# Turning q on quarters of TensorE's array: the first eight attention jobs of a fused retention and SwiGLU kernel

## The chip, the cores and the metric

The kernel runs on one core of one Trainium2 chip. A core has TensorE (matrix products; PE in the profile, PEld for its weight loads), VectorE (DVE), ScalarE (ACT), GpSimd (POOL) and SyncE (SP, which here only issues DMAs). The metric is device time in microseconds, as the median of several executions. Lower is better. Everything is fp32; one product is two passes through the array, and so two weight loads and two matmuls in the trace, and a transpose on TensorE is one of each.

## The reference

The first half is causal retention over 8 batches and 8 heads, with 576 tokens and 64 features a head. The second half is RMS-normalised SwiGLU over the 4608 tokens that result.

```python
scores = (1.0 / np.sqrt(D_)) * np.matmul(q, k.transpose(0, 1, 3, 2))
gamma = 1.0 - 2.0 ** (-5.0 - np.arange(H))
rel = pos[:, None] - pos[None, :]
Dmat = np.where(rel >= 0, gamma[:, None, None] ** rel[None, :, :], 0.0)
x = np.matmul(scores * Dmat, v)              # (B, H, S, D) -> (B*S, H*D) = (4608, 512)

xn = x / np.sqrt(np.mean(x * x, axis=-1, keepdims=True) + 1e-06) * rms_g
g = xn @ w_gate                              # 512 -> 1536
out = (g * (1.0 / (1.0 + np.exp(-g))) * (xn @ w_val)) @ w_out
```

## The kernel before

**Attention.** A job is one batch and one pair of heads (e = 0 and 1): 32 jobs, job j for batch j // 4. The pair fills the 128 partitions: 64 features of one head, 64 of the other. Retention is computed in chunks of 64 tokens, nine a job. The products of features need q and k with features on partitions (qT and kT), while memory has tokens on rows, so every job has to turn them.

For the jobs from the ninth on, `prepare` does that on VectorE. For the first eight, `turn(j)` does it on TensorE. The changed function is `turn`, with `load_tails`, which loads what it turns last. The 576 tokens of a head are four full tiles of 128 and a tail of 64:

- `load_first` loads the full tiles of q so that partition p holds tokens 4p to 4p + 3 of each head; those of k so that a tile has 128 consecutive tokens. Four lots of q, k and v go to free parts of `h`, the other four to free parts of `ring`.
- `load_tails` loads the tails of q, k and v of one or several heads into the tile `vi`, each on partitions 0 to 63 and in its own columns. `TAILS` has four such loads: heads 0 and 1 of batch 0 (issued by ScalarE's queue), the other six (by SyncE's), and the same for batch 1.
- `turn(j)` takes three PSUM banks. For q it multiplies each tile of each head by the identity (L236): 128 rows of the array and 64 columns, e choosing the column half. The result of tile c goes to every fourth column from c on, so that the tokens come out in order. For k it transposes the tiles of both heads at once (L230, 128x128). The two tails are transposed into a third bank (L245, 64 rows). ScalarE copies each of the four results to SBUF: two of 512 columns (L241), two of 64 (L252).

After `turn(j)` comes `slot(j)`, with TensorE's work in this order: `values(j-1)` (L379), `scores(j)` (L292), `states(j)` (L315) and `carried(j-1)` (L399). All of these are products of 64x64. `scores` puts the head on the row half of the array and the chunk's parity on the column half, so that four products are on four quarters, with a PSUM bank for each row half. `carried` adds to what `values` left, head e on the row half e and the column half e, and so uses two quarters. VectorE weights the scores with the decay (`weigh`, L328), sums the states (`sums`, L341) and scales what `carried` left into x (L425). ScalarE scales v (`scale_v`, L273), copies half of the states (L349) and computes squares for the norm (L458).

**Order.** The order of the first two units of 512 tokens is written out by hand in `PLAN`: T is `turn`, S is `slot`, V is `scale_v`, C is `close` (values and carried of the last of the eight jobs). N is `norm_1` (L481: means of squares, one column wide; then a power on GpSimd), D is `diagonals` (L495, ScalarE), X is `norm_2` (L546, which spreads the roots to all rows, and L548). U is `up_plain` (L704: products 512 columns wide with w_gate and w_val), and a and w are steps that make weights out of the 64-bit inputs on ScalarE and VectorE. The first steps are T0 V0 S0 T1 V1 S1 T2 and so on; N0 comes after S6, D0 after that and before T7, X0 after T7, then S7, the first U, C7. `LOADS` is the order of the DMAs; SyncE issues nearly all of them.

**The rest.** Later units (512 tokens each, from the third on) run their up- and down-projections as block products with fewer multiplications (`up`, L644; `across`, L814), with the weight blocks read back from DRAM into `ring`, and with jobs nine to 32 between them.

Of the kernel before, what the change touches and what calls it, by code (L numbers as in the profile page):

```python
# [10 lines left out]
F32 = mybir.dt.float32  # L11
# [3 lines left out]
P = 128  # L15
L = P // 2
# [28 lines left out]
def kernel(  # L45
# [11 lines left out]
    nc = tc.nc  # L57
    B, H, S, D = q.shape
    NTOK, DM = out.shape
    DFF = moe_w_gate.shape[1]  # L60
    NHP = H // 2
    NF = DFF // P
    NC = S // L
    NFULL = S // P
    TAIL = S - NFULL * P
# [16 lines left out]
    att = ctx.enter_context(tc.tile_pool(name="att", bufs=2))  # L82
# [6 lines left out]
    def bank(name):  # L89
        return banks.tile([P, 512], F32, tag="b", name=name)  # L90
# [13 lines left out]
    ident = const.tile([P, P], F32, name="ident")  # L104
# [18 lines left out]
    h = const.tile([P, NF, U], F32, name="h")  # L123
# [3 lines left out]
    NV = 4 * 7 * P  # L127
    vi = const.tile([P, NV + 2 * 4 * NK * P], F32, name="vi")
# [20 lines left out]
    st = [{} for _ in jobs]  # L149
# [33 lines left out]
    def load_tails(i, queue):  # L183

        b, heads = TAILS[i]
        for n, (nm, src) in enumerate((("qt", q), ("kt", k), ("vt", v))):
            at = NV + (3 * b + n) * DM
            t = vi[:TAIL, at : at + DM].rearrange("p (h d) -> p h d", d=D)
            cut = slice(heads[0], heads[-1] + 1)
            queue.dma_start(  # L190
                out=t[:, cut], in_=src[b, cut, NFULL * P :].rearrange("h p d -> p h d")
            )
            for hp in range(heads[0] // 2, heads[-1] // 2 + 1):
                st[b * NHP + hp][nm] = t[:, 2 * hp : 2 * hp + 2]

    def load_kv(j):

# [14 lines left out]
    def warm_up(n, width=P):  # L212

        if not warm_of:
            warm_of[0] = bank("warm")
        for _ in range(n):
            nc.tensor.matmul(
                warm_of[0][:, :width], lhsT=ones, rhs=ones[:, :1].to_broadcast([P, width]),
                start=True, stop=True,
            )  # L220

    def turn(j):

        d = st[j]
        n = NFULL
        for nm in "qk":
            ps = bank(f"turn_{j}_{nm}")
            for c in range(n):
                if nm == "k":
                    nc.tensor.transpose(  # L230
                        out=ps[:, c * P : c * P + P],
                        in_=d["k"][:, c].rearrange("p e d -> p (e d)"), identity=ident,
                    )
                    continue
                for e in range(2):
                    nc.tensor.matmul(  # L236
                        ps[side(e), c : n * P : n], lhsT=d["q"][:, e, c], rhs=ident,
                        start=True, stop=True,
                    )
            t = d[nm + "T"] = att.tile([P, S], F32, tag=nm + "T", name=f"{nm}T_{j}")  # L240
            nc.scalar.copy(out=t[:, : n * P], in_=ps[:, : n * P])  # L241
        last = bank(f"turn_{j}_t")
        for i, nm in enumerate("qk"):
            o = slice(i * TAIL, i * TAIL + TAIL)
            nc.tensor.transpose(  # L245
                out=last[:, o], in_=d[nm + "t"].rearrange("p e d -> p (e d)"),
                identity=ident[:TAIL, :TAIL],
            )
        warm_up(j == 0, 2 * P)
        for i, nm in enumerate("qk"):  # L250
            o = slice(i * TAIL, i * TAIL + TAIL)
            nc.scalar.copy(out=d[nm + "T"][:, NFULL * P :], in_=last[:, o])  # L252

    def prepare(j):

# [23 lines left out]
    def side(i):  # L279
        return slice(i * L, i * L + L)  # L280
# [304 lines left out]
    at = AT_SUMS  # L585
    for kind, u, n in pieces:
        size = UP if kind == "up" else OUT
        if at + size > RING:
            at = AT_SETS if kind == "out" and u < 2 else 0
# [754 lines left out]
```

## Time and profile before

| | |
|---|---|
| median of 3 runs | 1104.73 us (1101.4 to 1110.42) |
| span of the profiled execution | 1104.5 us, 24454 instructions |
| PE busy | 1091.5 us (99%), 10102 matmuls and as many loads |
| DVE, ACT, POOL busy | 751.7, 339.7, 458.0 us |
| granted clock of TensorE, mean | 0.995 |
| up to 57.38 us (first L704): PE busy | 50.51 us of 57.38, clock 0.91 |
| DMA moved | 243.60 MB, 221 GB/s in the mean |

The profile has no time of the profiled execution other than its span; the span lies 0.2 us under the median of the runs. A row of the timeline reads: start, time taken, engine, line, operation, written tile <- read tiles, shape of the array or operands, number of instructions, and in brackets the engine's idle time before it with what ended it. "issue" means that the engine waited for nothing that the profile shows. A matmul's row includes the time in which its result drains; the rate of a group is read from the starts of it and of the next.

Of a job's turn and slot in a stretch without stops (job 3, 23.27 to 27.85 us), TensorE spends 1.03 us on q's products, 0.59 on k's transposes, 0.26 on the tails', 0.55 on `values`, 0.63 on `scores`, 0.48 on `states` and 1.05 on `carried`.

### The profile page before, as it was taken

Reading aid. Unit: us, or ns where it says so; the run is one execution under the profiler, and the core shown is the slowest. Engines: PE = TensorE matmul, PEld = TensorE weight load, DVE = VectorE, ACT = ScalarE, POOL = GpSimd, SP = SyncE. Lnnn points to the kernel's source line nnn. Section 1 sums busy time; section 2 is a strip of 40 time slices with the busy share of each in tenths; the row PEclk is TensorE's granted clock in tenths of the full one; section 3 lists DMA queues with packets and bytes.
Section 4 is the critical chain, followed back from the end, with each engine's and each line's share of the span. In section 5 each row is a group of like instructions: output and inputs, shape, how many; then the busy total and the mean of one; then the engine's idle time right before and its main releaser. Section 6 shows DMA issues by size and latency. Waiting matters only on the chain.

```text
span 1104.5 us, 24454 instructions
## 1 busy us (share of the span) xinstructions
PE 1091.5 (99%) x10102; PEld 915.1 (83%) x10102; DVE 751.7 (68%) x1219; ACT 339.7 (31%) x757; POOL 458.0 (41%) x421
## 2 busy tenths in 40 slices
PE   8899999999999999999999999999999999999998
PEld 7654444479988899889988998889888998898898
DVE  3778568877866794678657775668565935594457
ACT  5855564331124412342034303330233111211110
POOL 0026325538430196027802581239321942393236
PEclk9899999999999999999999999999999999999999
DMA  8847777696978866787678865887475755585461
GB/s 211 197 139 259 280 244 217 208 343 185 289 277 227 216 251 226 185 238 235 253 215 199 285 259 149 245 246 284 143 203 198 273 193 176 183 293 158 152 247 43
DMA packets 253871, 243.60 MB, mean 221 GB/s; under 512 B 193216, under 2 KB 213824, under 8 KB 247616
## 3 DMA queue, kind: packets, MB, share of 16 engines
q1 hardware_dynamic: 252320, 241.64, 69.1%
q8 instruction: 79, 1.29, 0.5%
q10 hardware_dynamic: 1440, 0.40, 0.2%
q14 instruction: 32, 0.26, 0.1%
HBM read 211.92 MB, written 30.08 MB: 219 GB/s over the span
## 4 chain that ended last, share of the span: by engine, by line
PE 96%; DVE 1%; issue 1%; ACT 0%; POOL 0%; POOLq 0%; DVEq 0%; ACTq 0%
PE up L704 15%; PE x L644 14%; PE w L644 13%; PE z L644 13%; PE y L644 7%; PE xo L814 6%; PE xp L814 4%; PE zo L814 4%; PE zp L814 3%; PE wo L814 2%; PE yo L814 2%; PE av L379 2%; PE wp L814 2%; PE av L399 2%; PE s L292 2%; PE yp L814 2%
## 5 line engine op out<-in xcount | busy, mean ns | idle before, releaser
L704 PE MATMUL up<-x,ring 128*128 128x512 f32 x384 | 167.1, 595 | 0.0
L644 PE MATMUL x<-x,ring 128*128 128x256 f32 x672 | 161.1, 383 | 0.0
L644 PE MATMUL w<-sums,ring 128*128 128x256 f32 x672 | 158.9, 379 | 0.0
L644 PE MATMUL z<-x,ring 128*128 128x256 f32 x672 | 158.8, 379 | 0.0
L766 POOL TENSOR_TENSOR vi<-h 128x384 f32<-128x384 f32 x32 | 39.5, 1234 | 275.2 <-DVE h L663 266.3
L704 PEld LDWEIGHTS up<-x,ring 128*128 128x128 f32 x384 | 72.3, 190 | 89.3 <-issue 84.8
L644 PEld LDWEIGHTS z<-x,ring 128*128 128x128 f32 x672 | 127.8, 190 | 19.8 <-issue 2.9
L644 PEld LDWEIGHTS w<-sums,ring 128*128 128x128 f32 x672 | 127.7, 190 | 17.2
L644 PEld LDWEIGHTS x<-x,ring 128*128 128x128 f32 x672 | 125.5, 190 | 17.4 <-ACT m L670 0.2
L771 POOL TENSOR_TENSOR vi<-h 128x384 f32<-128x384 f32 (+2 forms) x46 | 46.4, 1009 | 149.5 <-DVE h L663 149.5
L1010 POOL TENSOR_TENSOR vi<-vi 128x512 f32<-128x512 f32 (+1 forms) x77 | 78.1, 1027 | 37.9 <-DVE vi L841 21.5
L644 PE MATMUL y<-sums,ring 128*128 128x256 f32 x336 | 79.4, 379 | 0.0
L670 ACT COPY m<-x 128x512 f32<-128x512 f32 x42 | 24.6, 586 | 173.4 <-PE x L644 173.4
L651 DVE TENSOR_TENSOR h<-u,w 128x512 f32<-128x512 f32 x42 | 28.9, 688 | 67.8 <-PE w L644 67.8
L651 DVE TENSOR_TENSOR u<-m,y 128x512 f32<-128x512 f32 x42 | 28.8, 687 | 63.4 <-PE y L644 62.7
L644 PEld LDWEIGHTS y<-sums,ring 128*128 128x128 f32 x336 | 63.9, 190 | 8.6
L665 ACT ACTIVATE h<-h 128x512 f32<-128x512 f32 x63 | 39.7, 630 | 84.1 <-DVE h L651 84.1
L1130 POOL TENSOR_TENSOR vi<-vi 128x512 f32<-128x512 f32 (+1 forms) x24 | 40.7, 1696 | 30.8 <-DVE vi L1119 17.3
L651 DVE TENSOR_TENSOR u<-u,z 128x512 f32<-128x512 f32 x42 | 28.9, 688 | 33.7 <-PE z L644 33.6
L1130 POOL TENSOR_TENSOR ring<-ring 128x512 f32<-128x512 f32 x24 | 30.4, 1272 | 49.3 <-DMA w_up_blocks<-ring 44.1
L771 POOL TENSOR_TENSOR vi<-vi,h 128x384 f32<-128x384 f32 (+2 forms) x46 | 47.6, 1034 | 3.6
L771 POOL TENSOR_TENSOR vi<-h,vi 128x384 f32<-128x384 f32 (+2 forms) x46 | 46.9, 1019 | 3.6
(314 smaller groups left out, 2086.5 us busy)
## 6 DMA issues: line engine op xcount, KB each, us to landing
ring<-w_out_blocks SPq DMA_DIRECT2D x59, 1344.0 KB, 6.4
ring<-w_up_blocks SPq DMA_DIRECT2D x42, 1792.0 KB, 7.7
w_out_blocks<-vi SPq DMA_DIRECT2D x21, 448.0 KB, 5.9
out_dram<-vi SPq DMA_DIRECT2D x64, 128.0 KB, 3.0
qraw<-in_q_dram SPq DMA_DIRECT2D x96, 72.0 KB, 5.1
kraw<-in_k_dram SPq DMA_DIRECT2D x96, 72.0 KB, 2.5
k<-in_k_dram SPq DMA_DIRECT2D x48, 128.0 KB, 2.9
v<-in_v_dram SPq DMA_DIRECT2D x48, 128.0 KB, 2.8
```

The source lines that it names most:

```text
L292: nc.tensor.matmul(s[e][side(odd), i * L : i * L + L], lhsT=d["kT"][side(e), c * L : c * L + L], rhs=d["qT"][side(e), c * L : c * L + L], ...
L379: mm = nc.tensor.matmul(av[odd][column(j, odd, e), i * L : i * L + L], lhsT=d["v"][side(odd), i, e] if c < NC - 1 else d["vt"][:, e], rhs= ...
L644: nc.tensor.matmul(ps[:, i * HU : i * HU + HU], lhsT=w[:, PLACE[blk], c, i * P : i * P + P], rhs=t_of[u][blk][:, c], start=(start and i == ...
L651: nc.vector.tensor_tensor(out=o, in0=a, in1=pairs_of(ps), op=ALU.add)
L665: nc.scalar.activation(out=o, in_=c, func=AF.Silu)
L670: nc.scalar.copy(out=s1, in_=pairs_of(x_))
L704: nc.tensor.matmul(ps, lhsT=w[:, PLACE[blk], c % 2, i * P : i * P + P], rhs=x_of[u][:, c], start=(c == 0), stop=(c == NHP - 1),)
L766: eng.tensor_tensor(out=i1, in0=x12, in1=x11, op=ALU.subtract)
L771: eng.tensor_tensor(out=o[:, c], in0=a[:, c], in1=b[:, c], op=op)
L814: nc.tensor.matmul(ps, lhsT=lhs[:, c], rhs=w[:, s, c], start=((nm, s // 4) not in first), stop=False, skip_group_check=True,)
L1010: eng.tensor_tensor(out=t[:, :, o], in0=t[:, :, x], in1=t[:, :, y], op=ALU.add)
L1130: nc.gpsimd.tensor_tensor(out=t[o], in0=t[x], in1=t[y], op=op)
```

## The change

- `load_tails` puts k's tail on partitions 64 to 127, in the same columns as q's tail, which stays on 0 to 63. The tile of both is called `qkt`. v's tail stays on partitions 0 to 63 in columns of its own. The DMAs are as many as before, of the same sizes, in the same order and on the same queues.
- `turn` multiplies q in 16 products of 64x64 instead of eight of 128x64: each tile of each head is split at partition 64 into two halves (r = 0 and 1), which take the two row halves of the array, while e takes the column half. The halves write to two PSUM banks, tokens 0 to 255 and 256 to 511.
- One 128x128 transpose of `qkt`, into the second bank behind q's columns, replaces the two of 64 rows. It stands between q's products and k's transposes; in the kernel before, the tails come last.
- k's transposes are the same, and now last. k has the third bank.
- ScalarE's copies all come behind the products in the program: 256 columns of q, then 320 (the other half of q and q's tail side by side), k's tail of 64, and k's 512.

```diff
@@ load_tails
-        for n, (nm, src) in enumerate((("qt", q), ("kt", k), ("vt", v))):
-            at = NV + (3 * b + n) * DM
-            t = vi[:TAIL, at : at + DM].rearrange("p (h d) -> p h d", d=D)
-            cut = slice(heads[0], heads[-1] + 1)
+        cut = slice(heads[0], heads[-1] + 1)
+        for n, (nm, src) in enumerate((("q", q), ("k", k), ("vt", v))):
+            at = NV + (2 * b + n // 2) * DM
+            t = vi[:, at : at + DM].rearrange("p (h d) -> p h d", d=D)
+            rows = side(n % 2)
             queue.dma_start(
-                out=t[:, cut], in_=src[b, cut, NFULL * P :].rearrange("h p d -> p h d")
+                out=t[rows, cut], in_=src[b, cut, NFULL * P :].rearrange("h p d -> p h d")
             )
             for hp in range(heads[0] // 2, heads[-1] // 2 + 1):
-                st[b * NHP + hp][nm] = t[:, 2 * hp : 2 * hp + 2]
+                part = t[:, 2 * hp : 2 * hp + 2]
+                if nm == "vt":
+                    st[b * NHP + hp][nm] = part[:TAIL]
+                else:
+                    st[b * NHP + hp]["qkt"] = part
@@ turn
-        for nm in "qk":
-            ps = bank(f"turn_{j}_{nm}")
-            for c in range(n):
-                if nm == "k":
-                    nc.tensor.transpose(
-                        out=ps[:, c * P : c * P + P],
-                        in_=d["k"][:, c].rearrange("p e d -> p (e d)"), identity=ident,
+        t = [bank(f"turn_{j}_q{r}") for r in range(2)]
+        for c in range(n):
+            for e in range(2):
+                for r in range(2):
+                    nc.tensor.matmul(
+                        t[r][side(e), c : n * L : n], lhsT=d["q"][side(r), e, c],
+                        rhs=ident[side(r), side(r)], start=True, stop=True,
                     )
-                    continue
-                for e in range(2):
-                    nc.tensor.matmul(
-                        ps[side(e), c : n * P : n], lhsT=d["q"][:, e, c], rhs=ident,
-                        start=True, stop=True,
-                    )
-            t = d[nm + "T"] = att.tile([P, S], F32, tag=nm + "T", name=f"{nm}T_{j}")
-            nc.scalar.copy(out=t[:, : n * P], in_=ps[:, : n * P])
-        last = bank(f"turn_{j}_t")
-        for i, nm in enumerate("qk"):
-            o = slice(i * TAIL, i * TAIL + TAIL)
+        m = n * L
+        nc.tensor.transpose(
+            out=t[1][:, m : m + P], in_=d["qkt"].rearrange("p e d -> p (e d)"), identity=ident
+        )
+        tk = bank(f"turn_{j}_k")
+        for c in range(n):
             nc.tensor.transpose(
-                out=last[:, o], in_=d[nm + "t"].rearrange("p e d -> p (e d)"),
-                identity=ident[:TAIL, :TAIL],
+                out=tk[:, c * P : c * P + P], in_=d["k"][:, c].rearrange("p e d -> p (e d)"),
+                identity=ident,
             )
         warm_up(j == 0, 2 * P)
-        for i, nm in enumerate("qk"):
-            o = slice(i * TAIL, i * TAIL + TAIL)
-            nc.scalar.copy(out=d[nm + "T"][:, NFULL * P :], in_=last[:, o])
+        qT, kT = (att.tile([P, S], F32, tag=nm, name=f"{nm}_{j}") for nm in ("qT", "kT"))
+        d["qT"], d["kT"] = qT, kT
+        nc.scalar.copy(out=qT[:, :m], in_=t[0][:, :m])
+        nc.scalar.copy(out=qT[:, m:], in_=t[1][:, : m + TAIL])
+        nc.scalar.copy(out=kT[:, n * P :], in_=t[1][:, m + TAIL : m + 2 * TAIL])
+        nc.scalar.copy(out=kT[:, : n * P], in_=tk)
```

## The prediction

> **What bounds the kernel now.** I read the page first (engines, slices, chain), then the waits, then TensorE's timeline of the stage that the change touches, then the queues and the clock of that stage.
>
> The page's line of busy times, and its line of the queue that brings TensorE's program:
>
> ```profile
> PE 1091.5 (99%) x10102; PEld 915.1 (83%) x10102; DVE 751.7 (68%) x1219; ACT 339.7 (31%) x757; POOL 458.0 (41%) x421
> ...
> q8 instruction: 79, 1.29, 0.5%
> ```
>
> TensorE is busy 1091.5 of 1104.5 us, and the chain that ended last is 96% PE: a microsecond that TensorE gains or loses early is kept to the end, unless something else holds it. From 57.38 to 1090 us it is idle for 1.9 us in all (1032.6 us long, 1030.7 busy, by the view of stretches), so only the time at which the first wide product (L704, at 57.38 us) starts has to be worked out. The second line: 79 blocks, 1.29 MB, 20204 loads and matmuls, so some 16 KB and 256 instructions to a block. The timeline of PE before 58 us:
>
> ```profile
> 13.26 0.27 PE L245 MATMUL turn_t<-ident,vi 64*128 64x64 f32 x1 [1.35 <-DMA vi<-in_k_dram]
> ...
> 25.15 0.69 PE L379 MATMUL av<-ret,h 64*64 64x64 f32 x32
> ...
> 29.52 0.76 PE L236 MATMUL turn_q<-ident,ring 128*64 128x128 f32 x9 [1.01 <-issue]
> ...
> 34.36 1.08 PE L399 MATMUL av<-qT,sum 64*64 64x64 f32 x29 [0.81 <-issue]
> ...
> 38.99 0.27 PE L292 MATMUL s<-qT,kT 64*64 64x64 f32 x1 [0.36 <-issue]
> ...
> 40.59 1.09 PE L236 MATMUL turn_q<-ident,ring 128*64 128x128 f32 x16
> 41.61 0.66 PE L230 MATMUL turn_k<-ident,ring 128*128 128x128 f32 x4
> 42.20 0.33 PE L245 MATMUL turn_t<-ident,vi 64*128 64x64 f32 x2
> ...
> 49.43 0.80 PE L236 MATMUL turn_q<-ident,ring 128*64 128x128 f32 x5 [1.32 <-issue]
> ...
> 51.61 2.08 PE L546 MATMUL rb<-diag,ones 128*128 128x512 f32 x2
> ...
> 57.38 3.70 PE L704 MATMUL up<-x,ring 128*128 128x512 f32 x8
> ```
>
> Four stops, 3.5 us, are "issue": TensorE waits for no engine and no data. Counted in the program's order (two loads and two matmuls for a product, one pair for a transpose, and waits that stand alone), they lie at instructions 1219, 1475, 1731 and 2243: exactly 256 apart, and 512 over one turn, at 1987, where the timeline has 0.1 us. TensorE stands at the end of a code block and the next is not there. The queues of 25.44 to 49.5 us:
>
> ```profile
> q1 hardware_dynamic: 13573, 5.06, 84.1%
> q8 instruction: 5, 0.08, 1.6%
> ```
>
> Five blocks in 24.0 us, behind loads that fill 84% of the engines. Turns stand at 20.76, 25.44, 29.52, 34.36, 38.99, 43.23 and 49.43 us; the packet of the next block starts 1.3 to 3.4 us after a turn (22.26, 27.13, 31.53, 36.50, 40.32, 46.64), takes 1.0 to 1.4 us, and TensorE goes on 1.2 to 1.6 us after its end. So a block takes 4.1, 4.8, 4.6, 4.2 and 6.2 us from 25.44 on, 4.8 in the mean. **From 25 to 49 us the arrival of code bounds the kernel, not the work of TensorE.**
>
> **TensorE's work, part by part.** q's turn now: 16 matmuls (eight products in two passes) from 40.59 to 41.61, 1.02 us. After: 16 products of 64x64 on quarters, 32 matmuls. The nearest rows are L379 and L292, on four quarters: 32 in 0.51 us (25.15 to 25.66), 16 ns each, so 0.50 us; the other end is L399, which keeps two quarters busy: 32 in 1.05 us, no gain. I take 0.50: the new order (two rows, then two columns, a bank for each row) is that of L292. Tails: two transposes in 0.26 us become one like k's, 0.59/4 = 0.15. Per job 1.02 - 0.50 + 0.26 - 0.15 = 0.63 us less; eight jobs, 5.0 us. A job's TensorE work falls from 4.58 to 3.95 us (q 0.50, tails 0.15, k 0.59, values 0.55, scores 0.63, states 0.48, carried 1.05).
>
> **Code.** q's instructions go from 32 to 64 a job, the tails' from 4 to 2: +30, over eight jobs 240, 0.94 of a block, at 4.8 us a block +4.5 us where blocks bound. That is nearly what the work saves. Between, the turns fall on other instructions, so I walk through them.
>
> **Start.** In job 1 TensorE waits for the k tail until 13.2 us either way (no load is moved), but k's four transposes now stand behind that wait, and behind them the values and scores: scores start at 13.26 + 0.15 + 0.59 + 0.1 + 0.58 (the copy of kT, now ScalarE's last) = 14.7 instead of 13.99. Job 0 loses some 0.5 us likewise (its k tail lands between 7.1, 3.07 + 4.0 of the q tail, and 7.5), hidden by job 1's wait. The 0.7 us of job 1 is covered by the block at turn 707, which is not there before 20.3 (packet 17.81 + 1.06 + 1.4); uncovered it would cost 0.7 once.
>
> **Walk.** With the block times of before at the nearest hour (4.0, 4.1, 4.8, 4.6, 4.4, 5.7, 4.4), the turns are at 20.4, 24.4, 28.5, 33.3, 37.9, 42.3, 48.0 and 52.4. Between turns lies 256/358 of a job, 2.8 us of work, so each ends in a stop of 1 to 2 us, except the last, which has norm_1's ms (1.9 us) in it. They fall in job 1's values and carried, job 3's states, job 4's scores, job 5's q, job 4's carried, job 6's scores, job 7's tails. After 52.4: k 0.59. rb (L546) needs the diagonals, in before ready 2.85 us after ms ends (47.3, then this row of ScalarE's timeline to 50.14):
>
> ```profile
> 48.88 1.26 ACT L495 ACTIVATE diag<-ident,r 128x128 f32<-128x128 f32 x4
> ```
>
> ms now ends near 51.6, diagonals at 54.5: job 7's shorter turn no longer covers this. rb 0.9 to 2.0 (full and half clock), then values, scores, states, carried 2.7 to 3.8: L704 starts between 58.1 and 60.3, minus what a quicker block gives; I take 58.9, **1.5 us later than 57.38**.
>
> **Edits at nothing.** The four copies of a job move 512+64 columns of q and k as before (0.58 + 0.58 + 0.22 + 0.23 us now; about 0.38 + 0.43 + 0.22 + 0.58 by the same slope), 1.6 us each way. Scores used to start before the tails' copies; now they await kT's copy, 0.1 us after the values end, hidden by the stops; uncovered 0.15 x 8 = 1.2 us. Three banks before and after; those of q and k were last read by ScalarE's copies of the job before or by VectorE's L328, both microseconds earlier. The tails' DMAs keep number, size and queue.
>
> **Two rules.** The four stops of 3.5 us are the row for code. The Trainium skill, "Runtime: NRT & Kernel Launch", Instruction fetch mechanics, says that code comes in 16 KiB blocks of 256 instructions, as counted here, and that crossing a boundary is mostly hidden, which the stops contradict. By it the sum would be the saving alone, 1099.7.
>
> The windows of before for the clock; in each row length, PE busy, four other engines, granted clock, DMA:
>
> ```profile
> 11.60:15.00 3.40, 2.02 (x84) 1.65 (x83) 0.76 (x4) 2.16 (x8) 0.09 (x1) 1.00 0.66 168
> 15.00:18.40 3.40, 3.40 (x68) 3.28 (x70) 2.56 (x8) 0.54 (x2) 0.00 (x0) 0.50 1.07 299
> ...
> 32.10:35.50 3.40, 2.35 (x88) 2.01 (x82) 3.33 (x9) 3.37 (x10) 0.00 (x0) 1.00 0.80 169
> ...
> 45.70:49.10 3.40, 2.41 (x26) 2.16 (x26) 3.22 (x11) 1.74 (x5) 1.02 (x1) 1.00 0.82 148
> 49.10:52.60 3.50, 3.17 (x12) 1.90 (x12) 1.72 (x3) 2.92 (x9) 0.00 (x0) 0.51 0.82 161
> ```
>
> After 2.02 us busy the next window has clock 0.50, after 2.41 (ms, one column wide) 0.51; after 2.35 the clock stays 1.00. So a stop of 1.3 us can cost the next window half its work. "TensorE: Matmul & The Clock Gate", Part 1, asks for an idle window of 3.4 us before the clock halves. By it no stop here would cost anything; the rows disagree.
>
> **The rivals.** *Faster: blocks come sooner.* If each took 4.1 us, the least of the bound stretch, the last turn is at 49.1, 3.3 earlier, and L704 starts near 55.6 to 56.5; if stops stay as long as they are, the whole 5.0 is gained. Gain 1 to 5 us, 1099.7 to 1103.7. For it: 4.1 and 4.2 occur; against: a turn that comes sooner meets the same loads. 0.22.
> *Slower: the half clock.* Longer stops empty the windows, and 3.4 us at half clock lose 1.7 us of work. Between turns that is free while 2.8 us of work at half clock (5.6) fits the block's 4.8, and decides from there on: past 48 us no block hides it. One more such window there, with blocks at 4.84 and one at 6.2 (+3.0 in all on the walk): 3 to 6.5 us, 1108 to 1111. 0.16.
> *The quarters don't overlap.* Then q takes 1.05, a job 4.5 us, 3.2 between turns: still less than a block, and the total as forecast. It is no case of its own.
> *The forecast*, 0 to 3 us later: 0.6. Neither side of 1%: 0.02 left.
>
> **The numbers.** The profiled execution's span is 1104.5, the median of the runs shown 1104.73: 0.2 apart, so + 1.5 gives 1106.2. The range takes in -5.0 (1099.7) and +6.5 (1111.2), with the runs' own scatter (1101.4 to 1110.42) no wider than that: 1099.5 to 1111.5. One per cent, 11 us, is about what a measurement of this kernel tells from no change; no case reaches it alone, so faster 0.03, same 0.92, slower 0.05.
>
> **What would show it.** Right: 32 q matmuls in 0.5 us; "issue" stops of 1 to 2 us at the eight places named, 256 instructions apart, in sum over 8 us; an rb that waits for the diagonals; L704's first product at 58 to 60 us. Wrong: the turns of code under 4.2 us apart and L704 at 53 us; or a clock of 0.5 in windows after 56 us; or q's matmuls at 33 ns.

## The result, and the profile after

The changed kernel takes **1112.11 us** (median of 12 runs, 1108.56 to 1113.86), the kernel before 1105.55 us (12 runs beside it, 1101.40 to 1110.42): a ratio of **1.0052, 95% interval [1.0039, 1.0064]** (the two medians alone would give 1.0059). Small, but clear of 1. Set on the 1104.73 us of the forecast, the ratio makes 1110.5 us (1109.0 to 1111.8): 5.7 us later, where the forecast said 1.5. The plain median lies 0.6 us above the top of the forecast's range; the ratio's centre lies inside it.

The profiled execution took 1109.76 us, its span 1108.0 us, 3.5 us more than the span of before. In this kernel the lines behind `turn` stand three further down: q L235, tail L240, k L245, scores L295, states L318, values L382, carried L402, ms L484, rb L549, first wide product L707. The page's line of busy times and its line of TensorE's program:

```profile
PE 1088.5 (98%) x10222; PEld 912.7 (82%) x10222; DVE 751.8 (68%) x1219; ACT 339.3 (31%) x757; POOL 458.9 (41%) x421
...
q8 instruction: 80, 1.31, 0.5%
```

120 more loads, 120 more matmuls, one more code block, 3.0 us less of busy PE. All the rest of the story lies ahead of the first wide product. In the view of stretches, from there to the end, the columns being length, busy time (and number) of PE, PEld, DVE, ACT and POOL, granted clock, DMA share and GB/s, the changed kernel has

```profile
60.80:1108.00 1047.20, 1041.30 (x8846) 873.30 (x8842) 717.14 (x1124) 301.81 (x660) 456.21 (x407) 1.00 0.69 221
```

The kernel before has 1047.10 and 1041.01 for the same stretch (57.40 to 1104.50). So the span is longer by what the first wide product is later: 60.85 against 57.38. The timeline of PE in the changed kernel, up to that product:

```profile
13.44 0.30 PE L240 MATMUL turn_q<-ident,vi 128*128 128x128 f32 x1 [2.44 <-DMA vi<-in_k_dram]
...
20.57 0.51 PE L382 MATMUL av<-ret,h 64*64 64x64 f32 x20 [1.51 <-issue]
...
33.55 0.81 PE L295 MATMUL s<-qT,kT 64*64 64x64 f32 x40 [0.78 <-ACT ring L276]
...
37.84 0.38 PE L235 MATMUL turn_q<-ident,ring 64*64 64x64 f32 x9 [1.61 <-issue]
...
47.79 0.40 PE L295 MATMUL s<-qT,kT 64*64 64x64 f32 x11 [1.81 <-issue]
...
49.58 1.95 PE L484 MATMUL ms<-mean_w,sq 128*128 128x1 f32 x16
...
51.45 0.69 PE L235 MATMUL turn_q<-ident,ring 64*64 64x64 f32 x32
52.08 0.33 PE L240 MATMUL turn_q<-ident,vi 128*128 128x128 f32 x1
...
54.68 2.08 PE L549 MATMUL rb<-diag,ones 128*128 128x512 f32 x2 [1.45 <-ACT diag L498]
...
56.69 1.13 PE L382 MATMUL av<-ret,ring 64*64 64x64 f32 x32
...
60.85 3.70 PE L707 MATMUL up<-x,ring 128*128 128x512 f32 x8
```

Four readings. The 32 matmuls of q take 0.63 us (51.45 to 52.08) where 16 took 1.02: the quarters do overlap. The k tail now holds up job 1 for 2.44 us instead of 1.35, since k's transposes stand behind it. The stops called "issue" have grown. And the stretch from rb to the first wide product takes 6.17 us, of which values to carried take 4.16 (56.69 to 60.85), though these need some 2.7 us in a stretch at full clock. The waits of PE up to 60 us (total, times, longest, in us):

```profile
PE turn_q L240 <- DMA vi<-in_k_dram: 3.1, 2, 2.4
PE s L295 <- issue: 1.8, 1, 1.8
PE turn_q L235 <- issue: 1.6, 1, 1.6
PE av L382 <- issue: 1.5, 1, 1.5
PE rb L549 <- ACT diag L498: 1.5, 1, 1.5
```

"issue" comes to 5.4 us (with 0.5 at the states), 3.5 before. The queues from 25.45 to 47.8 us, and ScalarE's diagonals, which in before were ready ahead of rb:

```profile
q1 hardware_dynamic: 11736, 5.07, 86.9%
q8 instruction: 5, 0.08, 1.3%
```

```profile
53.35 1.28 ACT L498 ACTIVATE diag<-ident,r 128x128 f32<-128x128 f32 x4 [0.16 <-POOL r L490]
```

The diagonals end at 54.63 us, rb starts at 54.68. Last, the clock in windows of 3.4 us (columns as in the stretch above):

```profile
19.00:22.40 3.40, 1.27 (x68) 1.06 (x65) 1.47 (x5) 0.75 (x3) 0.09 (x1) 1.00 0.53 122
22.40:25.80 3.40, 3.10 (x74) 2.91 (x76) 1.26 (x4) 2.40 (x9) 0.00 (x0) 0.50 0.77 146
...
36.10:39.50 3.40, 1.79 (x60) 1.42 (x50) 3.29 (x10) 2.72 (x10) 0.00 (x0) 0.99 1.07 261
39.50:42.90 3.40, 3.38 (x101) 3.15 (x97) 3.10 (x9) 2.29 (x7) 0.09 (x1) 0.50 0.76 155
...
49.70:53.10 3.40, 3.24 (x53) 2.85 (x53) 2.64 (x9) 1.51 (x3) 1.19 (x1) 1.00 0.56 90
53.10:56.50 3.40, 1.95 (x4) 0.50 (x2) 1.81 (x3) 3.21 (x11) 0.21 (x1) 0.50 0.85 179
56.50:59.90 3.40, 3.40 (x114) 3.22 (x115) 3.11 (x5) 1.86 (x3) 0.09 (x1) 0.50 0.72 185
```

A window that PE fills for 1.27 or 1.79 us is followed by one at half clock, twice; the third time the clock falls behind a window of which 1.83 us are ms (L484, one column wide), and it stays at half for a second window; in the first of the two rb waits for the diagonals, and PE is busy for 1.95 us. That makes 13.6 us at half clock; the kernel before has 10.2 (15.0 to 18.4 and 49.1 to 55.9).

**The sum of the profiled pair.** From its first matmul (at 1.22 us in both) to the first wide product TensorE is idle for 12.39 us, 5.66 before: +6.7. Saved work: -5.0, the forecast's figure. Half clock: 3.4 us more of it, +1.7. Together +3.4; measured +3.47. The busy time of PE up to that product falls from 50.5 to 47.2 us, by the 3.3 that -5.0 and +1.7 leave.

**The sum over all runs.** The profiled execution is one of the quicker ones of its kernel, 2.4 us under its median. All runs with a span on record took 1.7 to 2.0 us longer than the span, so the profiled execution of before, span 1104.5 us, took some 1106.3 by that, 0.8 above its median (1105.55). Hence the pair of profiles shows 3.5 us where the medians show 6.6. What separates the runs of the changed kernel is mostly the clock. Take as clock lost in a run (1 - mean granted clock) x time. Over the 12 runs of the changed kernel it is **8.1 us** in the mean, and a run is 0.88 us longer for each microsecond of it; its two runs at clock 0.995 take 1108.56 and 1109.53 us, the seven at 0.991 or 0.992 take 1111.58 to 1113.86. The kernel before loses 3.0 to 3.9 us (in the four sets of 14 to 29 runs taken with the experiments below). So 4.2 to 5.1 us more are lost; at 0.88 us each, 3.7 to 4.5 of the 5.7 us are clock, and 1.2 to 2.0 are the rest. That division is arithmetic on the records, and the slope is this kernel's (the four sets of before give 0.3 to 0.8); the experiments test it.

### The profile page after: what moved, and what is told of

The parts are those of the page before. It is cut to its first block, busy times and chain, and to the rows that moved or that the text cites. A ratio compares the mean times of both kernels' runs of the same rounds, so it can differ in the third digit from the quotient of the medians.

```text
span 1108.0 us, 24694 instructions
## 1 busy us (share of the span) xinstructions
PE 1088.5 (98%) x10222; PEld 912.7 (82%) x10222; DVE 751.8 (68%) x1219; ACT 339.3 (31%) x757; POOL 458.9 (41%) x421
## 4 chain that ended last, share of the span: by engine, by line
PE 94%; SPq 2%; DVE 1%; DMA 1%; issue 1%; POOL 0%; ACT 0%; POOLq 0%; DVEq 0%; ACTq 0%
PE up L707 15%; PE x L647 13%; PE w L647 13%; PE z L647 13%; PE y L647 7%; PE xo L817 6%; PE xp L817 4%; PE zo L817 4%; PE zp L817 3%; PE wo L817 2%; PE yo L817 2%; PE av L382 2%; PE wp L817 2%; PE s L295 2%; PE yp L817 2%; PE av L402 1%
## 5 line engine op out<-in xcount | busy, mean ns | idle before, releaser
L707 PE MATMUL up<-x,ring 128*128 128x512 f32 x384 | 167.1, 594 | 0.0
L769 POOL TENSOR_TENSOR vi<-h 128x384 f32<-128x384 f32 x32 | 39.5, 1236 | 274.5 <-DVE h L666 265.7
L707 PEld LDWEIGHTS up<-x,ring 128*128 128x128 f32 x384 | 72.2, 190 | 89.3 <-issue 85.1
L1013 POOL TENSOR_TENSOR vi<-vi 128x512 f32<-128x512 f32 (+1 forms) x77 | 78.2, 1029 | 37.9 <-DVE vi L844 21.4
```

Of the source, the lines that this page charges most:

```text
L707: nc.tensor.matmul(ps, lhsT=w[:, PLACE[blk], c % 2, i * P : i * P + P], rhs=x_of[u][:, c], start=(c == 0), stop=(c == NHP - 1),)
L769: eng.tensor_tensor(out=i1, in0=x12, in1=x11, op=ALU.subtract)
L1013: eng.tensor_tensor(out=t[:, :, o], in0=t[:, :, x], in1=t[:, :, y], op=ALU.add)
```

## The experiments

The theories: **clock** (the stops that the change leaves empty TensorE's windows, and the half clock behind them takes back more than was saved), **code** (240 more instructions cost their block, whatever the clock does), and **order** (the tail ahead of k, and so the wait in job 1). Each kernel was timed against the kernel before on the same chip. "First wide" is the start of the first wide product in the kernel's profile; "rb to wide" the time from the start of rb to it; "lost" the clock lost in a run, in the mean over its runs.

| kernel | ratio to before, 95% | lost, us | first wide, us | rb to wide, us |
|---|---|---|---|---|
| before | 1 | 3.0 to 3.9 | 57.38 | 5.77 |
| after | 1.0052 [1.0039, 1.0064] | 8.1 | 60.85 | 6.17 |
| joined_tails | 0.9987 [0.9978, 0.9995] | 2.3 | 54.14 | 4.70 |
| quarters | 1.0032 [1.0019, 1.0046] | 5.8 | 58.53 | 5.77 |
| wide_fill | 1.0026 [1.0014, 1.0039] | 2.6 | 59.47 | 3.66 |
| narrow_fill | 1.0046 [1.0029, 1.0063] | 6.8 | 63.86 | 6.33 |
| fill_job1 | 1.0067 [1.0052, 1.0082] | 8.4 | 63.59 | 6.01 |
| before_fill | 1.0022 [1.0010, 1.0034] | 1.7 | 60.18 | 3.76 |
| more_code | 1.0020 [1.0008, 1.0032] | 3.0 | 58.76 | 4.00 |
| more_work | 1.0012 [1.0001, 1.0022] | 4.1 | 58.31 | 4.58 |
| tail_last | 1.0039 [1.0020, 1.0058] | 5.7 | 62.45 | 6.25 |
| moved_halves | 1.0053 [1.0035, 1.0070] | 5.9 | 59.64 | 6.67 |
| q_two_loads | 1.0024 [1.0014, 1.0034] | 5.5 | 61.87 | 5.31 |
| q_transposed | 1.0064 [1.0047, 1.0081] | 8.7 | 59.49 | 5.81 |

### The two parts alone

**joined_tails**: the kernel before, with the tails loaded into one tile and turned by one transpose, last in `turn` as they were; q as before. 13 instructions fewer up to the first wide product.

```diff
...
         last = bank(f"turn_{j}_t")
-        for i, nm in enumerate("qk"):
-            o = slice(i * TAIL, i * TAIL + TAIL)
-            nc.tensor.transpose(
-                out=last[:, o], in_=d[nm + "t"].rearrange("p e d -> p (e d)"),
-                identity=ident[:TAIL, :TAIL],
-            )
+        nc.tensor.transpose(
+            out=last[:, :P], in_=d["qkt"].rearrange("p e d -> p (e d)"), identity=ident
+        )
```

> One part alone: q is turned as before (eight products of 128x64, one bank), the tails of q and k by the one transpose from one tile, last as before. TensorE's instructions before the first wide product: 2537 (before 2550, changed kernel 2792). If the arrival of code is what costs, this part is worth 13 instructions and 0.11 us a job, most of it inside stops: ratio to before 0.998 to 1.000. If the joined tile or its load is what made the changed kernel slower, it shows here: 1.004 or more.

Measured: 1104.03 us (12 runs) against 1105.23 (29 runs), 0.9987 [0.9978, 0.9995]: a little quicker than both kernels, 1.4 us. In its profile TensorE is idle for 4.8 us before the first wide product and has one window at half clock.

**quarters**: the kernel before, with q on quarters into two banks; the tails in two transposes, last, as before. 255 instructions more.

```diff
-        for nm in "qk":
-            ps = bank(f"turn_{j}_{nm}")
...
+        t = [bank(f"turn_{j}_q{r}") for r in range(2)]
+        for c in range(n):
+            for e in range(2):
+                for r in range(2):
                     nc.tensor.matmul(
-                        ps[side(e), c : n * P : n], lhsT=d["q"][:, e, c], rhs=ident,
-                        start=True, stop=True,
+                        t[r][side(e), c : n * L : n], lhsT=d["q"][side(r), e, c],
+                        rhs=ident[side(r), side(r)], start=True, stop=True,
                     )
...
+                out=t[1][:, m + i * TAIL : m + i * TAIL + TAIL],
+                in_=d[nm + "t"].rearrange("p e d -> p (e d)"), identity=ident[:TAIL, :TAIL],
```

> The other part alone: q by 16 products on quarters into two banks, the tails of q and k loaded and turned one by one and last, so that k's transposes in job 1 don't stand behind the k tail's load. 2805 instructions before the first wide product. If the arrival of code and the stops it makes are what costs, it is as slow as the changed kernel: 1.004 to 1.007. If the new order (k behind the tail) costs, it is near the saving of work alone: 0.996 to 0.999.

Measured: 1108.08 us (11 runs), 1.0032 [1.0019, 1.0046]. This lies between the two ranges expected. The loss lies in the quarters, the gain in the joined tails. It also shows that the order of tail and k is not needed for a loss. What is left between 1.0032 and the 1.0052 of both parts together (the joined tails should have taken some away) can be the order; see tail_last.

### The clock

**wide_fill**: the changed kernel with one product of 512 columns per job ahead of the tail. It writes k's bank, which k's transposes then overwrite: 32 instructions, 7 us of work that nothing needs.

```diff
         m = n * L
+        tk = bank(f"turn_{j}_k")
+        nc.tensor.matmul(
+            tk, lhsT=ones, rhs=ones[:, :1].to_broadcast([P, 512]), start=True, stop=True
+        )
         nc.tensor.transpose(
             out=t[1][:, m : m + P], in_=d["qkt"].rearrange("p e d -> p (e d)"), identity=ident
         )
-        tk = bank(f"turn_{j}_k")
```

> The changed kernel with one product of ones more in each of the eight jobs, 128x128 by 512 columns, between q's products and the tails' transpose, into the bank that k's transposes overwrite: 0.87 us of TensorE work more a job at full clock (7 us in all), 4 instructions a job. If TensorE's work bounded the stage, 1.0052 becomes 1.011 to 1.012. If code bounds it and nothing else, the work falls into the stops: 1.005 to 1.0065. If the half clock after the stops is the larger part of the loss, the filler keeps the clock up and gains 2 to 4 us: 1.001 to 1.004.

Measured: 1107.50 us (12 runs), 1.0026 [1.0014, 1.0039]. Seven microseconds of work more, and 2.9 us *less* than the changed kernel by the ratios. 2.6 us of clock are lost in a run instead of 8.1.

**narrow_fill**: the same, with a product of one column. Both fills have the same number of instructions in the same places, and so every code block begins at the same product in both.

```diff
-            tk, lhsT=ones, rhs=ones[:, :1].to_broadcast([P, 512]), start=True, stop=True
+            tk[:, :1], lhsT=ones, rhs=ones[:, :1], start=True, stop=True
```

> The changed kernel with one product per job of one column in place of the 512 columns of the kernel that was 1.0026 (wide_fill): the same 32 instructions at the same places, so every code block begins at the same product, but less than 1 us of added work in all instead of 7. If the filled kernel was quicker than the changed one because its added work kept TensorE's clock up, this one stands where the changed kernel stands, 1.004 to 1.007, with 6 us or more of clock lost in a run. If it was quicker because the code blocks begin at other products, this one is as quick or quicker, 1.0015 to 1.003, with some 2.6 us lost.

Measured: 1110.75 us (6 runs), 1.0046 [1.0029, 1.0063], 6.8 us lost. Without the columns the clock is lost again, so it was not the places of the code blocks that kept it up. The clocks of the two fills' runs hardly overlap (ten of the twelve runs of wide_fill have a mean clock of 0.996 or more, five of the six of narrow_fill 0.994 or less). Their times do: 1.0046 and 1.0026 are 0.0020 apart, and by the widths of the intervals 0.0021 would be clear of noise. Against the changed kernel wide_fill is clear, 0.0026 apart where 0.0018 would do. PE's timeline near the end of the stage, first wide_fill:

```profile
55.81 1.02 PE L552 MATMUL rb<-diag,ones 128*128 128x512 f32 x2
56.77 0.69 PE L385 MATMUL av<-ret,ring 64*64 64x64 f32 x32
...
59.47 3.70 PE L710 MATMUL up<-x,ring 128*128 128x512 f32 x8
```

and narrow_fill:

```profile
57.53 2.08 PE L552 MATMUL rb<-diag,ones 128*128 128x512 f32 x2 [1.62 <-ACT diag L501]
59.54 1.13 PE L385 MATMUL av<-ret,ring 64*64 64x64 f32 x32
...
63.86 2.41 PE L710 MATMUL up<-x,ring 128*128 128x512 f32 x5
```

In the one, two rb take 1.0 us, the 32 matmuls of the values 0.63 (56.77 to the scores at 57.40), and the first wide product is 3.66 us behind rb. In the other, rb has waited for the diagonals, as in the changed kernel; it takes 2.0 us, and the wide product is 6.33 us behind it. The profiles show more than the runs: narrow_fill's is its slowest execution (1112.01 us), wide_fill's lies under its median (1107.11).

**before_fill**: the kernel before with the same product of 512 columns per job, ahead of q's.

```diff
-        for nm in "qk":
-            ps = bank(f"turn_{j}_{nm}")
+        both = [bank(f"turn_{j}_{nm}") for nm in "qk"]
+        nc.tensor.matmul(
+            both[0], lhsT=ones, rhs=ones[:, :1].to_broadcast([P, 512]), start=True, stop=True
+        )
+        for nm, ps in zip("qk", both):
```

> The kernel before with the same product of 512 columns per job ahead of k's transposes: 7 us of work and 34 instructions. It loses only 3 us to the clock in a run, so by the clock theory there is little to win back: some of the added work shows, 1.001 to 1.005. If the added product is worth its time for another reason than the clock (the places of the code blocks, or the waits that follow it), the kernel before gets quicker as well, 0.996 to 1.000.

Measured: 1107.95 us (8 runs), 1.0022 [1.0010, 1.0034], 1.7 us lost. Here the filler is not worth its time: there were only 3.3 us of clock to win back.

**fill_job1**: the changed kernel with two such products in job 1 alone, in front of the tail for which TensorE waits there.

```diff
         m = n * L
+        tk = bank(f"turn_{j}_k")
+        for _ in range(2 * (j == 1)):
+            nc.tensor.matmul(
+                tk, lhsT=ones, rhs=ones[:, :1].to_broadcast([P, 512]), start=True, stop=True
+            )
...
-        tk = bank(f"turn_{j}_k")
```

> The changed kernel with two products of ones (512 columns, 1.7 us) in job 1 alone, between q's products and the tails' transpose, inside the 2.4 us in which TensorE waits for the k tail; 8 instructions. If job 1's idle time is what halves the clock, most of what the filler in all jobs gained (1.0052 to 1.0026) comes back here: 1.0025 to 1.0035, with 2 to 4 us less clock lost than 8.1. If the stops of the code in the later jobs halve it, this stays at 1.004 to 1.0055 and the clock lost at 6.5 us or more.

Measured: 1113.28 us (6 runs), 1.0067 [1.0052, 1.0082], 8.4 us lost. A miss for the idea that job 1's wait is what costs the clock: the wait shrank from 2.44 to 0.17 us (at 13.24), and there were windows at half clock all the same (21.5, 31.8, 45.4, and 55.7 for 6.8 us). The changed kernel's own profile says it too: the windows that hold this wait (8.7 to 12.1 and 12.1 to 15.6, PE busy for 2.06 and 2.16 us) are each followed by 1.00. What matters comes later, at the code's stops and the diagonals.

### Code or work

**more_code**: the kernel before with eight products of 64x64 and one column per job, 32 instructions each time: 251 more up to the first wide product, at most 2 us of work.

```diff
-        for nm in "qk":
-            ps = bank(f"turn_{j}_{nm}")
+        both = [bank(f"turn_{j}_{nm}") for nm in "qk"]
+        for i in range(8):
+            r, e = i % 2, i // 2 % 2
+            nc.tensor.matmul(
+                both[r][side(e), :1], lhsT=ident[side(r), side(r)],
+                rhs=ident[side(r), :1], start=True, stop=True,
+            )
+        for nm, ps in zip("qk", both):
```

> The kernel before with eight products more at the head of each of the eight turns: on quarters, with the identity, one column wide, into columns that the turn overwrites. 32 instructions a job, 251 in all before the first wide product (2801 instead of 2550; the changed kernel has 2792), and little work: 16 matmuls of one column, at most 16 ns each by the rows of the other products on quarters, 0.25 us a job, 2 us in all. If the arrival of code and the stops that it makes (with the half clock behind them) are the cause, it is as slow as the quarters or the changed kernel: 1.003 to 1.006. If the cause is in the work, the banks, the copies or the tails of the changed turn, at most 1.002.

**more_work**: the kernel before with one product of 128x128 per job, the same work in 29 instructions.

```diff
-        for nm in "qk":
-            ps = bank(f"turn_{j}_{nm}")
+        both = [bank(f"turn_{j}_{nm}") for nm in "qk"]
+        nc.tensor.matmul(both[0][:, :P], lhsT=ident, rhs=ident, start=True, stop=True)
+        for nm, ps in zip("qk", both):
```

> The control: the kernel before with one product of 128x128 by 128 columns more at the head of each turn, into columns that the turn overwrites: 0.25 us of work a job, as the last one's, in 4 instructions (2579 before the first wide product). By the code theory 0.11 of a block and work that the stops hide: 0.999 to 1.002. If 0.25 us of work a job is what makes the other slow, both are alike.

Measured: more_code 1107.32 us (12 runs), 1.0020 [1.0008, 1.0032]; more_work 1106.03 (12 runs), 1.0012 [1.0001, 1.0022]; before 1105.05 (23 runs). Both cost something, and the two are not told apart: the price of a code block is not settled by these times. The 1.0020 lies below the 1.003 to 1.006 expected if code decides, though the interval touches it. The trace of more_code settles another thing. It has nearly as many instructions as the changed kernel (2801 against 2792 to the first wide product) and up to 7 us more of work (the 5.0 that the change saves and at most 2 added). From 29 us on its code turns stand at 29.58, 33.64, 37.78, 42.02, 47.52 and 52.94 us; those of the changed kernel at 29.31, 33.57, 37.85, 42.15, 47.80 and 52.74. **In this pair the pace is that of the code; work taken away goes into stops.** The pace is no constant of the code, though. In the profiles of wide_fill and narrow_fill every code block begins at the same product, narrow_fill has less work, and yet from 29 us on its turns are 1 to 3 us later (30.7 to 54.6 against 29.6 to 52.4 us); it has two windows at half clock ahead of 52 us, wide_fill none. That those made the difference is likely, not shown. PE's timeline of more_code from there on:

```profile
49.39 1.95 PE L487 MATMUL ms<-mean_w,sq 128*128 128x1 f32 x16
...
51.61 1.77 PE L242 MATMUL turn_q<-ident,ring 128*64 128x128 f32 x16
53.31 1.12 PE L236 MATMUL turn_k<-ident,ring 128*128 128x128 f32 x4
...
54.76 1.36 PE L552 MATMUL rb<-diag,ones 128*128 128x512 f32 x2
56.05 0.70 PE L385 MATMUL av<-ret,ring 64*64 64x64 f32 x32
...
58.76 3.70 PE L710 MATMUL up<-x,ring 128*128 128x512 f32 x8
```

ms at nearly the same time (49.39 against 49.58), rb too (54.76 against 54.68). But q's 16 matmuls (1.7 us, the clock is at half here) and k's fill the time in which the diagonals are made; rb waits for nothing, the clock returns during it (two rb in 1.29 us, the values in 0.63), and the first wide product comes at 58.76: 2.1 us ahead of the changed kernel, and 4.00 us behind rb instead of 6.17. Over its runs more_code loses 3.0 us of clock, no more than the kernel before.

### The order

**tail_last**: the changed kernel with the tail's transpose behind k's, and ScalarE's copies in that order.

```diff
-        nc.tensor.transpose(
-            out=t[1][:, m : m + P], in_=d["qkt"].rearrange("p e d -> p (e d)"), identity=ident
-        )
         tk = bank(f"turn_{j}_k")
...
+        nc.tensor.transpose(
+            out=t[1][:, m : m + P], in_=d["qkt"].rearrange("p e d -> p (e d)"), identity=ident
+        )
...
```

> The changed kernel with the tails' transpose moved behind k's transposes, and ScalarE's copies in the order q, k, second half of q with its tail, k's tail. The same instructions (2793 before the first wide product), so the same code and the same work. If the place of the tail is what separates the changed kernel (1.0052) from the quarters alone (1.0032), because job 1 idles 2.4 us in one piece and the next window of TensorE's clock is halved, this gives 1.002 to 1.0035 and less clock lost than the changed kernel's 8.1 us a run (5 to 6.5). If code alone decides, it stays at 1.0045 to 1.006.

Measured: 1111.24 us (7 runs, 1106.29 to 1114.31), 1.0039 [1.0020, 1.0058]. The interval holds both the 1.0052 of the changed kernel and the 1.0032 of quarters. The clock lost, 5.7 us instead of 8.1, is as expected if the order matters, but the mean clocks of its seven runs reach from 0.989 to 0.998. Inconclusive: whether the order costs anything stays open.

### Turning q with less code

**moved_halves**: the changed kernel, with q turned by four transposes of 128x128 (two tiles of one head at a time) and the halves put into place by four ScalarE copies of 64 rows and 256 columns. 2346 instructions, 204 fewer than before.

```diff
+        for e in range(2):
+            for i in range(2):
+                nc.tensor.transpose(
+                    out=t[e][:, i : 2 * P : 2],
+                    in_=d["q"][:, e, 2 * i : 2 * i + 2].rearrange("p t d -> p (t d)"),
+                    identity=ident,
+                )
...
+        for e in range(2):
+            for odd in range(2):
+                nc.scalar.copy(out=qT[side(e), odd : n * P : 2], in_=t[e][side(odd), :m])
...
```

> The changed kernel with q turned by four transposes of 128x128 instead of 16 products: each takes two tiles of one head, and ScalarE's copies (four of 64x256) bring the halves to their partitions. Loads as in the changed kernel. TensorE's work a job is 0.59 us for q instead of 0.50, ScalarE's some 0.9 us more; TensorE's instructions before the first wide product 2346 instead of 2792, 1.75 blocks of code fewer. If TensorE's work or the number of products on quarters bounded the stage, nothing is gained on the changed kernel, and ScalarE's longer copies cost up to 0.9 us a job: 1.005 to 1.011. If code bounds it, 1.75 blocks of 4.8 us less: 8 us less than the changed kernel, less what the copies cost: 0.996 to 1.000.

Measured: 1110.87 us (6 runs), 1.0053 [1.0035, 1.0070], in the range for the copies' cost and a miss for the idea that less code makes it quicker. The code's stops shrink to 1.1 us, but TensorE now waits for ScalarE, seven times (PE's waits up to 60 us):

```profile
PE s L297 <- ACT kT L257: 7.7, 7, 1.6
```

**q_two_loads** (a control) and **q_transposed**: joined_tails with q loaded by one DMA per head, so that both heads of a token lie side by side, in pieces of 256 bytes; then, in q_transposed, q turned by four transposes like k's. 2345 instructions.

```diff
-            st[j]["q"] = room.rearrange("p (e t d) -> p e t d", e=2, d=D)
-            nc.sync.dma_start(
-                out=room.rearrange("p (e t) -> p e t", e=2),
-                in_=src.rearrange("e (p t) d -> p e (t d)", p=P),
-            )
+            q_ = st[j]["q"] = room.rearrange("p (t e d) -> p t e d", e=2, d=D)
+            for e in range(2):
+                nc.sync.dma_start(
+                    out=q_[:, :, e], in_=src[e].rearrange("(p t) d -> p t d", p=P)
+                )
...
+                nc.tensor.transpose(
+                    out=ps[:, c : n * P : n] if nm == "q" else ps[:, c * P : c * P + P],
+                    in_=d[nm][:, c].rearrange("p e d -> p (e d)"), identity=ident,
+                )
```

> The control of the next one: the kernel with the joined tails alone (0.9987), with q of the first eight jobs loaded by two DMAs a job so that the two heads of a token lie side by side (pieces of 256 bytes instead of 1 KB), and turned by eight products as before. Code and work are those of the joined tails. The loads are eight more, and smaller: 0.998 to 1.004, all of the difference from 0.9987 the loads'.

> The same loads, with q turned by four transposes of 128x128: 8 instructions a job for q instead of 32 (before) or 64 (quarters); 2345 before the first wide product. TensorE's work for q is 0.59 us a job, more than the quarters' 0.50. If work decided, this could not beat the quarters by more than the tails' order: 1.003 or more, and about the control less 3 us at best. If code and the stops that it makes decide, the turns of blocks fall from 10 or 11 to 9 before the first wide product, the stops of 'issue' nearly vanish, and it lies 3 to 6 us under the control and 6 to 9 us under the quarters: 0.994 to 0.998.

Measured: q_two_loads 1108.90 us (12 runs), 1.0024 [1.0014, 1.0034]; q_transposed 1112.93 us (6 runs), 1.0064 [1.0047, 1.0081]. A miss. In the profiles q_transposed does reach its first wide product 2.4 us before its control (59.49 against 61.87), with 1.9 us of stops for code; but it meets its loads instead (PE's waits up to 60 us):

```profile
PE turn_t L241 <- DMA vi<-in_k_dram: 3.1, 2, 1.8
PE turn_q L234 <- DMA ring<-in_q_dram: 2.3, 2, 1.8
```

Behind the first wide product its profile loses 5.6 us against the kernel before (1052.7 us to the end instead of 1047.1). Its trace has 3.2 us more of waits there (the longest, 2.1 us at 295.7, for a ScalarE copy, L824) and one window at half clock behind that one (297.1 to 300.5, at most 1.7 us); what delayed the copy isn't settled. The profiles of moved_halves and q_transposed suggest that in this stage code, loads and ScalarE's copies are nearly level: with less of the one, the next holds.

## Why the prediction was right, and where it was wrong

**Right: what bounds the stage, and where its turns fall.** The forecast put the turns of code at 20.4, 24.4, 28.5, 33.3, 37.9, 42.3, 48.0 and 52.4 us. They came at 20.58, 25.45, 29.31, 33.57, 37.85, 42.15, 47.80 and 52.74: within 0.4 us but for the second and third, which are 1.0 and 0.8 late (the window from 22.4 to 25.8 is at half clock). That the saved work would go into stops is what the profile shows, and more_code, with more work at the same pace, agrees with it.

**Right: q and the tail.** 32 matmuls in 0.63 us where 0.50 was taken and 1.05 was the other end; the tail by the same transpose as k's. From the second matmul of `carried` to the first of `values`, both at full clock, the turn now takes 2.24 us (16.38 to 18.62) instead of 2.95 (22.20 to 25.15 before): 0.71 less a job, where 0.63 was forecast.

**Half right: the stops for code.** Sum forecast over 8 us, at eight places. The profile calls 5.4 us "issue", at four of them: 1.5 to 1.8 us at three, 0.5 at one. At 33.55, a fifth, the 0.78 us of idle time are put down to ScalarE (L276). All idle time between the first matmul and the first wide product makes 12.4 us.

**Right: the diagonals.** Forecast at 54.5 us, ready at 54.63; rb waited for them as said.

**Wrong: the last term of the walk, from rb to the first wide product.** The forecast took "rb 0.9 to 2.0 (full and half clock), then values, scores, states, carried 2.7 to 3.8" and, between 58.1 and 60.3, chose 58.9: 4.4 us. Measured: 2.0 + 4.16 = 6.17, above the upper end. The kernel before had this stretch in its own trace, rb at 51.61 and L704 at 57.38, 5.77 us; with that row the forecast would have been 60.3, +2.9 (the pair of profiles has +3.5). Choosing 4.4, it counted on 1.4 us that the clock did not give. The stretch was at half clock before, and the wait for the diagonals, which the same paragraph foresaw, takes busy time out of the window in which the clock could have returned. In the 14 profiles, of the windows at half clock up to the first wide product, all 24 with 3.14 us or more of busy PE were followed by full clock, all seven with 2.61 or less by another at half; between, both occur. The changed kernel's window with the wait has 1.95. The kernel before's in its place has 3.13 and was followed by half clock too, so without the wait the clock need not have come back. more_code shows that 58.76, the forecast's number almost, is what the same code takes if rb doesn't wait.

**Too low a chance: the rival of the half clock.** "3 to 6.5 us, 1108 to 1111", at 0.16, is what the ratio says (5.7 us). The forecast's own case, 0 to 3 us later at 0.6, did not come; the range holds the result only because it reached as far as this rival. For a forecast of 1.5 us that is luck. The rival's reason was right, its place was not the only one: it had one more window at half clock past 48 us, and the profile has the same 6.8 us there as before and, ahead of it, two windows (22.4 and 39.5, behind stops of 1.5 and 1.6 us) where before has one (15.0). What the forecast lacked altogether is that the clock differs from run to run. The profiled execution of before, at 0.995, had more than its kernel's usual share of half clock already (5.4 us lost by that figure, 3.0 to 3.9 in the mean), so the pair of profiles shows less of the difference than the runs do: 3.0 to 3.9 us lost before, 8.1 after. The forecast's 0.2 us between span and median compared unlike things, since a run takes 1.7 to 2.0 us longer than its span. That the idle time lowers the clock, and is not a mere companion, is shown by wide_fill against narrow_fill: the same code, 2.6 us lost with the work and 6.8 without. That this costs time is shown by wide_fill against the changed kernel: 7 us more of work, and 1.0026 instead of 1.0052.

**The rule on the clock.** The Trainium skill, "TensorE: Matmul & The Clock Gate", Part 1, asks for an idle window before the clock halves. The rows of the changed kernel again differ: windows with 1.27 and 1.79 us of busy PE were followed by 0.50. They give no simple threshold of busy time either: 46.30 to 49.70, with 1.91 us, was followed by 1.00. In the 14 profiles, of the windows at full clock up to the first wide product that hold less than 0.5 us of ms, all six with 1.53 us or less of busy PE were followed by 0.50 and none with more than 2.12; between, both occur. (These windows are laid from the recorded starts of the half clock, 3.41 us each; those of the rows are rounded.)

**Left open.** Why both parts together (1.0052) lose more than the quarters alone (1.0032), when the joined tails alone gain: the order is one candidate, and tail_last could not decide. And what a code block costs by itself: 251 instructions with at most 2 us of work cost 2.2 us in more_code (0.9 to 3.5 by the interval), and the same work in 29 instructions 1.3 (0.1 to 2.4). The forecast's 4.5 us for 240 instructions isn't what either shows by itself.

## What to carry to other kernels

In a stage that is paced by something else (here the arrival of TensorE's code behind heavy loads), taking work off TensorE may gain nothing, and may lose: the idle time that it makes can lower the granted clock, and the work that follows pays. Price a stretch at the end of such a stage by its own row in the trace, at the clock that it had, and not by the rate of a quiet stretch; then ask whether the change fills or empties the window before it. The saving that also removed instructions (one transpose for two) gained here; the one that doubled them (quarters for whole tiles) lost.

## What the runs showed that was not expected

- Work that nobody needs can make a kernel quicker: 7 us of products took the changed kernel from 1.0052 to 1.0026. Where less clock was lost to begin with (before_fill, 3.3 us) the same products, at the head of the turn, cost 2.4 us.
- The changed kernel's runs differ by the clock: 0.88 us for each microsecond of lost clock, and most of its spread of 5.3 us. In other sets of runs the slope is smaller (0.3 to 0.8 in those of before).
- ms, 16 matmuls of one column in 1.95 us, keeps PE busy in the profile but seems not to keep up the clock: in before (45.7 to 49.1) and after (49.7 to 53.1) the window that holds it is followed by 0.51 and 0.50, though PE was busy for 2.41 and 3.24 us. So it is in 13 of the 14 profiles. In q_two_loads it is not, so the one-column products alone don't decide it (columns as above, the next window below):

```profile
50.30:53.70 3.40, 3.40 (x57) 3.28 (x52) 0.89 (x3) 1.30 (x4) 0.00 (x0) 1.00 0.99 338
53.70:57.10 3.40, 1.51 (x11) 0.82 (x7) 3.15 (x11) 3.37 (x10) 1.02 (x1) 1.00 0.87 180
```
